# q and k in nine passes of 128 outputs, and an instruction order that counts blocks of 128 pairs

## The chip, the cores and the metric

The kernel runs on one core of a Trainium2 chip. The metric is the time of one execution on the device in microseconds; for a kernel, the median of several executions is given with the lowest and the highest. The core's engines have their own instruction streams: TensorE (PE) for matrix products, with its weight loads (PEld) beside it, VectorE (DVE), ScalarE (ACT), GpSimd (POOL) and SyncE (SP), which here issues most of the DMAs in the order in which they stand in its queue.

## The reference

Four layers on x of 2048 rows and 576 columns, each with a layer norm ahead of it and a residual sum behind it: attention A, mixer B, and both again with the same weights.

```python
def _A_ref(x, wqkv, wo):
    H = 32; Dh = D // H          # 18
    W, dil = (8, 2)
    qkv = (x @ wqkv).reshape(B, S, 3, H, Dh).transpose(2, 0, 3, 1, 4)
    q, k, v = (qkv[0], qkv[1], qkv[2])
    idx = pos[:, None] - (jnp.arange(W) * dil)[None, :]
    ...
    logits = jnp.einsum('bhsd,bhswd->bhsw', q, kg) * Dh ** (-0.5)
    attn = _softmax(jnp.where(mask, logits, -1e9))
    o = jnp.einsum('bhsw,bhswd->bhsd', attn, vg)
    return o.transpose(0, 2, 1, 3).reshape(B, S, D) @ wo
def _B_ref(x, w_in, w_sp, b_sp, w_out):
    z = _gelu(jnp.einsum('bsd,df->bsf', x, w_in))          # 4608 columns
    z1 = z[..., :Fh]
    z2 = _layernorm(z[..., Fh:], axis=-1)
    g = jnp.einsum('ts,bsf->btf', w_sp, z2) + b_sp[None, :, None]
    return jnp.einsum('bsf,fd->bsd', z1 * g, w_out)
x = x + _A_ref(_layernorm(x), A_wqkv, A_wo)
x = x + _B_ref(_layernorm(x), B_w_in, B_w_sp, B_b_sp, B_w_out)
x = x + _A_ref(_layernorm(x), A_wqkv, A_wo)
x = x + _B_ref(_layernorm(x), B_w_in, B_w_sp, B_b_sp, B_w_out)
```

A row attends to eight rows: itself and those 2, 4, ... 14 above it.

## The kernel before

There are five stages, `phase_F(0)`, `phase_S(1)`, `phase_F(2)`, `phase_S(3)` and `phase_E()`. An F stage (an attention stage, below) makes the attention layer and the half z2 of the mixer's first product, with its norm. An S stage makes z1 (`z1_ps`) and the spatial product (`g_ps`). The mixer's last product (`p_ps`, `p3_steps`) is done at the start of the following F stage, or in E for the last layer.

In an F stage the normalised input lies transposed in `xnD`: features on the partitions, in five chunks along `NM + 1`. The first four chunks are 128 features each. The last has 64 features, and they stand twice, in rows 0 to 63 and again in rows 64 to 127, so that two products of half the array's height can run side by side. That is what `mm576` does: for two outputs `s` it issues four full chunks each (8 matmuls, L246) and the half chunk of each (2 matmuls, L240), the half chunks first or last, so that two neighbours that use `mm576` can share one change between full and half height.

Attention goes over 18 tiles of 114 rows (each with a halo of 14 rows above it, 128 in all), and 9 groups of two tiles. For a group, `QK_steps` makes q and k with the outputs (32 heads of 18 = 576 each) on the partitions and the group's 242 rows as columns. It goes in five pieces `d` of 126, 126, 126, 126 and 72 outputs, seven heads or four; a piece holds q in one half of a PSUM tile `H` and k in the other. DVE or ACT copies a piece to a buffer `stg` with even and odd rows apart (`.e`), SP writes it to `qk_bounce` in DRAM (`.w`), and when all five pieces are written, four DMAs read it back as `QK` with heads side by side at partitions 0, 32, 64 and 96. Three tiles `H` in PSUM serve every matrix product of the stage in turn.

A tile then goes: `L_ps`, the logits, two steps of 32 small matmuls (18 rows, 57 columns, L516); exp on ACT (L524); the mask on DVE (L531); `O_ps`, 64 small matmuls (L539) with v (`v_ps`, 20 matmuls, L485); the division on DVE (L548); five transposes `o_tp`; `w_ps`, ten matmuls with wo (L588); the residual sum on DVE (L593); its store, its layer norm (statistics on DVE, three small operations on POOL, the scaling on ACT L277) and five transposes `ln_tp` back into `xnD`. The z2 half (`z_ps`, from L246 and L240) of 128 rows is three `mm576` steps, gelu on ACT, squares on DVE and ACT, small operations on POOL and a scaling on DVE.

Which step follows which on an engine is written out by a planner when the kernel is built. `Flow.step` records a step with its engine, an assumed cost, a due time `key`, the steps it needs (`after`) and the buffers it takes; `Flow.order` then places the steps one at a time, each time on the engine that is free first, and there the ready step with the lowest due time. Due times are tile numbers less constants in `Plan`, one set for each attention stage: `KQ` for q and k, `KV` for v, `KL` for the logits, and so on; `LX`, `LW` and `LR` are the assumed latencies of loads, of the write to `qk_bounce` and of its read. The emitted order is fixed: an engine that waits for one step holds all that stand behind it, on SP too. PE's steps in the stage are not emitted in any other order than the planner's.

Of the kernel before, what the change touches and what calls it, by code (L numbers as in the profile page):

```python
# [9 lines left out]
ACT = mybir.ActivationFunctionType  # L10
# [31 lines left out]

Plan = namedtuple("Plan", "LX LW LR KQ KX KV KL KE KM KP KF KY KZ STAY")
PLANS = (Plan(LX=6.05, LW=5.23, LR=6, KQ=5.82, KX=8.97, KV=1.81, KL=2.17, KE=1.72, KM=1.23, KP=0.96, KF=1.71, KY=1.13,
              KZ=16, STAY=0.41),
         Plan(LX=3.13, LW=3.88, LR=7.8, KQ=4.18, KX=10.88, KV=0.84, KL=1.2, KE=1.46, KM=0, KP=0.42, KF=0.82, KY=1.35,
              KZ=13.51, STAY=0.39))
# [3 lines left out]
class Flow:  # L51
# [4 lines left out]

    LAG = 0.12
    SWITCH = dict(PE=0.1, ACT=1.3)

    def __init__(self, caps, stay=0.6):  # L60
        self.caps, self.stay = caps, stay
        self.steps = []
        self.by = {}
        self.users = {}

    def step(self, name, eng, cost, key, fn, after=(), uses=(), takes=(), mode=None, lag=None):
        st = dict(name=name, eng=eng if isinstance(eng, tuple) else (eng,), cost=cost, key=key, fn=fn,
                  after=list(after), takes=takes, mode=mode, lag=self.LAG if lag is None else lag, n=len(self.steps))
# [26 lines left out]

    def order(self):
# [5 lines left out]
        while left:  # L102
            best = {}
            for st in left.values():
# [5 lines left out]
                else:  # L110
# [3 lines left out]
                    t = max(t, tk)  # L114
                    e = min(st["eng"], key=lambda e: max(free.get(e, 0.0), t))
# [21 lines left out]
            free[e] = st["end"]  # L137
            for tag, b in st["takes"]:
                taken.setdefault(tag, []).append(b)
# [14 lines left out]
class K:  # L154
# [7 lines left out]
    def __init__(self, ctx, tc, aps):  # L162
# [3 lines left out]
        self.dma_rr = 0  # L166

# [83 lines left out]
    def ln_steps(self, fl, tag, key, row0, n, x, after, uses=(), guard=()):  # L251
# [41 lines left out]
        fl.step(tag + ".t", "PE", 0.32, key, trans, [tag + ".n"], [tag + ".xn"], takes=[("PT", tag + ".tp")], mode="w")  # L293
# [9 lines left out]
    def p3_steps(self, fl, i, key, wout, x_prev, li, after=()):  # L303
# [35 lines left out]
        for hh in range(2):  # L339
            for part in range(2):  # L340
# [3 lines left out]
                        takes=[("H", tag + ".ps")] if (hh, part) == (0, 0) else [], mode="w")  # L344
# [12 lines left out]
    def phase_F(self, li):  # L357
# [11 lines left out]
        fl = Flow(dict(H=3, PT=2, QK=3, bn=2, stg=6, x=nx, xw=3, xn=3, ln_st=6, o_t=2, oT=2, xb=8), pl.STAY)  # L369
# [5 lines left out]
        wqk = pool.tile([P, NM, 2, D], bf16, name="wqk")  # L375
        wqk_r = pool.tile([P, D], bf16, name="wqk_r")
# [23 lines left out]
        def load_qk():  # L400
            self.load576(lambda s: wqk[:, :, s, :], wqk_r, self.A_wqkv[:, 0:D], self.A_wqkv[:, D:2 * D], (nc.sync,))
# [29 lines left out]
        def QK_steps(g, key):  # L431
# [5 lines left out]
            for d in range(5):  # L437
                M = 126 if d < 4 else 72

                def mm(rest_first, d=d, M=M):  # L440
                    ps = box[d] = self.Ht("qk_ps")
                    cols, at = slice(126 * d, 126 * d + M), slice(c0, c0 + gw)
                    self.mm576(lambda s: ps[:M, s, 0:gw], rest_first,
                               lambda s, c: (wqk[:, c, s, cols], self.xnD[:, c, at]),
                               lambda s, rows: (wqk_r[rows, cols], self.xnD[rows, NM, at]))

                def ev(e, d=d, M=M):
                    t = pool.tile([P, 4 * GH], bf16, name="stg", bufs=6)
                    stg = box[d, "s"] = t[:, 0:2 * gw].rearrange("p (q r j) -> p q r j", q=2, r=2)
                    self.copy(e, stg[:M], box[d][:M, :, 0:gw].rearrange("p q (j r) -> p q r j", r=2))  # L450

                def wr(_, d=d, M=M):
                    self.dma(box["bn"][126 * d:126 * d + M], box[d, "s"][:M])
                fl.step(f"{tag}.m{d}", "PE", 0.2 + 0.0039 * gw, key, mm, feeds(c0, gw) + ["wqk"],
                        takes=[("H", f"{tag}.ps{d}")], mode="wn")
                fl.step(f"{tag}.e{d}", ("DVE", "ACT"), dict(DVE=0.15 + 0.00215 * gw, ACT=0.15 + 0.0018 * gw), key, ev,
                        [f"{tag}.m{d}"], [f"{tag}.ps{d}"],
# [253 lines left out]
        with tc.manual_schedule():  # L711
            fl.issue()
# [134 lines left out]
```

## Time and profile before

| what | value |
|---|---|
| median of 3 executions | 1275.97 us (1269.72 to 1276.37) |
| the profiled execution, time | 1273.12 us |
| its span, first to last instruction | 1271.4 us |
| mean granted TensorE clock | 0.987 |
| first attention stage, to the first `z1_ps` | 0 to 245.3 us |
| first S stage | 245.3 to 565.9 us |
| second attention stage, with `p_ps` at its start | 565.9 to 874.6 us |
| second S stage and E | 874.6 to 1271.4 us |
| PE busy in the two attention stages | 230.5 of 245.3 us, 300.1 of 308.7 us |
| DVE and ACT busy in the second attention stage | 188.1 us and 159.2 us |
| share of the 16 DMA engines in the two attention stages | 0.53 and 0.49 |

A window's line has its length, the busy time of each engine with its number of instructions in brackets, the mean granted clock of PE (1.00 is full speed), the share of the DMA engines that was busy, and GB/s. In the page's groups a line of code comes with its engine, its operation, its shapes and count, the busy time with the mean duration of one, and the idle time ahead of it with what ended it. A duration of a matmul is longer than the distance to the next one, since they are pipelined; the distance is read from start to start in the timeline.

### The profile page before, as it was taken

Reading aid. Unit: us, or ns where it says so; the run is one execution under the profiler, and the core shown is the slowest. Engines: PE = TensorE matmul, PEld = TensorE weight load, DVE = VectorE, ACT = ScalarE, POOL = GpSimd, SP = SyncE. Lnnn points to the kernel's source line nnn. Section 1 sums busy time; section 2 is a strip of 40 time slices with the busy share of each in tenths; the row PEclk is TensorE's granted clock in tenths of the full one; section 3 lists DMA queues with packets and bytes.
Section 4 is the critical chain, followed back from the end, with each engine's and each line's share of the span. In section 5 each row is a group of like instructions: output and inputs, shape, how many; then the busy total and the mean of one; then the engine's idle time right before and its main releaser. Section 6 shows DMA issues by size and latency. Waiting matters only on the chain.

```text
span 1271.4 us, 27781 instructions
## 1 busy us (share of the span) xinstructions
PE 1239.1 (97%) x12182; PEld 730.5 (57%) x12244; DVE 551.9 (43%) x897; ACT 408.9 (32%) x658; POOL 201.4 (16%) x494
## 2 busy tenths in 40 slices
PE   7999999999999999999999998999999999999998
PEld 5788765444444444448788886554444444444576
DVE  5866665433222232334467675654233232322311
ACT  6566687600111111103333446875110011111011
POOL 5311157600000000002111112674000000000000
PEclk9999899999999999999999898999999999999999
DMA  7655319150000000044554455049300000000232
GB/s 192 159 149 163 95 48 199 29 129 10 10 10 10 10 10 1 1 140 147 140 141 115 113 142 161 18 105 197 83 1 10 10 10 10 10 1 2 82 101 68
DMA packets 142877, 96.31 MB, mean 76 GB/s; under 512 B 92084, under 2 KB 127604, under 8 KB 142756
## 3 DMA queue, kind: packets, MB, share of 16 engines
q1 hardware_dynamic: 142068, 92.17, 28.1%
q0 software_dynamic: 688, 2.38, 0.7%
q8 instruction: 95, 1.56, 0.5%
q14 instruction: 26, 0.21, 0.1%
HBM read 51.19 MB, written 26.55 MB: 61 GB/s over the span
## 4 chain that ended last, share of the span: by engine, by line
PE 92%; DMA 2%; ACT 2%; issue 1%; DVE 1%; POOL 0%; SPq 0%; DVEq 0%; POOLq 0%; ACTq 0%
PE g_ps L764 39%; PE z_ps L246 20%; PE p_ps L321 10%; PE qk_ps L246 6%; PE w_ps L588 4%; PE v_ps L485 3%; PE z_ps L240 3%; PE O_ps L539 3%; PE L_ps L516 1%; DMA QK<-qk_bounce 1%; PE ln_tp L283 1%; PE qk_ps L240 1%; PE o_tp L568 1%; ACT P L524 1%; DMA wqk<-in_A_wqkv_dram 1%
## 5 line engine op out<-in xcount | busy, mean ns | idle before, releaser
L764 PE MATMUL g_ps<-W,zu 128*128 128x512 bf16 x2256 | 497.7, 379 | 2.5
L764 PEld LDWEIGHTS <-zu 128*128 128x128 bf16 x2304 | 225.4, 98 | 271.9
L769 DVE TENSOR_TENSOR g_tmp<-g_ps,bsp 128x512 f32<-128x512 f32 x144 | 99.0, 687 | 437.6 <-PE g_ps L764 437.6
L759 ACT ACTIVATE zu<-z_ps 128x1024 bf16<-128x1024 f32 x72 | 73.7, 1024 | 514.4 <-PE z_ps L240 477.1
L246 PE MATMUL z_ps<-xnD,w 128*128 128x512 bf16 x562 | 132.1, 379 | 1.2 <-issue 0.6
L321 PEld LDWEIGHTS <-zu 128*128 128x128 bf16 x1152 | 111.6, 98 | 30.6 <-DVE zu L770 2.1
L246 PE MATMUL z_ps<-wA,xnD 128*128 128x384 bf16 x576 | 109.8, 327 | 0.1
L321 PE MATMUL p_ps<-wA,zu 128*128 128x288 bf16 x768 | 106.7, 286 | 0.0
L770 DVE TENSOR_TENSOR zu<-g_tmp,zu 128x512 bf16<-128x512 f32 x144 | 99.7, 692 | 9.9 <-DVE g_tmp L769 0.5
L246 PEld LDWEIGHTS <-xnD 128*128 128x128 bf16 x768 | 70.8, 98 | 56.5 <-issue 14.4
L246 PEld LDWEIGHTS <-w 128*128 128x128 bf16 x576 | 52.8, 97 | 75.2 <-issue 15.7
L246 PE MATMUL qk_ps<-xnD,wqk 128*126 128x242 bf16 (+1 forms) x720 | 90.4, 272 | 1.8 <-ACT xnD L301 0.9
L633 ACT ACTIVATE zu<-z_ps 128x768 bf16<-128x768 f32 x96 | 77.4, 806 | 35.8 <-PE z_ps L240 20.1
L643 DVE CUSTOM_DVE_ANT_1 zu<-zu 128x1536 bf16<-128x1536 bf16 x32 | 56.6, 1769 | 55.0 <-ACT zu L633 55.0
L246 PEld LDWEIGHTS <-wqk 128*126 128x126 bf16 (+1 forms) x720 | 75.1, 133 | 8.6 <-issue 6.6
L524 ACT ACTIVATE P<-L_ps 128x912 bf16<-128x912 f32 x72 | 64.8, 944 | 18.9 <-PE L_ps L516 18.8
L266 POOL TENSOR_SCALAR ln_st<-ln_st 128x1 f32<-128x1 f32 (+1 forms) x68 | 18.8, 277 | 315.6 <-DVE ln_st L262 273.4
L328 DVE TENSOR_TENSOR x<-p_ps,x 128x576 f32<-128x576 f32 x32 | 24.2, 757 | 90.6 <-PE p_ps L321 90.6
L588 PE MATMUL w_ps<-wo,oT 128*114 128x288 bf16 (+1 forms) x360 | 56.5, 309 | 0.4 <-ACT P L524 0.2
L277 ACT ACTIVATE xn<-xw,ln_st 114x512 bf16<-114x512 f32 (+1 forms) x72 | 43.0, 646 | 33.5 <-POOL ln_st L268 33.2
L300 DVE CAST stg<-qk_ps 126x484 bf16<-126x484 f32 (+1 forms) x61 | 40.3, 660 | 28.5 <-PE qk_ps L240 14.6
L588 PEld LDWEIGHTS <-oT 128*114 128x114 bf16 (+1 forms) x360 | 47.1, 142 | 4.0 <-issue 1.7
(79 smaller groups left out, 1116.1 us busy)
## 6 DMA issues: line engine op xcount, KB each, us to landing
QK<-qk_bounce SPq DMA_DIRECT2D x72, 136.1 KB
x<-xres SPq DMA_DIRECT2D x32, 288.0 KB
xres<-xw SPq DMA_DIRECT2D x34, 256.5 KB
qk_bounce<-stg SPq DMA_DIRECT2D x72, 119.1 KB
w<-in_B_w_in_dram SPq DMA_DIRECT2D x36, 128.0 KB
xres<-x SPq DMA_DIRECT2D x16, 288.0 KB
xw<-xres SPq DMA_DIRECT2D x17, 256.5 KB
wA<-in_B_w_in_dram SPq DMA_DIRECT2D x12, 288.0 KB
```

Of the source, the lines that this page charges most:

```text
L240: nc.tensor.matmul(ps(s), lhsT=lhsT, rhs=rhs, start=first, stop=not first)
L246: nc.tensor.matmul(ps(s), lhsT=lhsT, rhs=rhs, start=(c == 0 and not rest_first), stop=(c == NM - 1 and rest_first))
L277: nc.scalar.activation(out=out, in_=in_, func=ACT.Identity, scale=rstd[:n], bias=nmr[:n])
L321: nc.tensor.matmul(ps[:, hh, 0:288], lhsT=u[:, s * S + i * P:s * S + (i + 1) * P], rhs=wout(b, s)[:, hh * 288:(hh + 1) * 288], start=(b == ...
L524: nc.scalar.activation(out=Psb[:, 2 * hh:2 * hh + 2, :, 0:QH], in_=box["L", hh][:, :, 0:8 * QH].rearrange("p a (b c) -> p a b c", c=QH), f ...
L588: nc.tensor.matmul(box["ps"][:n, hh, 0:288], lhsT=box["oT"][:, c, :n], rhs=wo[:, c, hh * 288:(hh + 1) * 288], start=(c == 0), stop=(c == 4))
L633: nc.scalar.activation(out=self.zu[:, 3 * u:3 * u + 3, 256 * i:256 * (i + 1)].rearrange("p j (s r) -> p s j r", s=2), in_=box[u][:, :, 0:3 ...
L643: nc.vector.tensor_tensor_reduce(out=junk(0, 6), in0=z[:, 0:6, :], in1=z[:, 0:6, :], scale=1.0 / FH, scalar=0.0, op0=ALU.mult, op1=ALU.add ...
L759: nc.scalar.activation(out=u[:, :, 512 * q:512 * (q + 1)], in_=ps[:], func=ACT.Gelu_apprx_tanh)
L764: nc.tensor.matmul(ps[:, s, :], lhsT=z2[:, i, s, :], rhs=W[q][:, i, :], start=(i == 0), stop=(i == NS - 1))
L769: nc.vector.tensor_tensor(out=tmp[:], in0=ps[:, s, :], in1=bsp[:, 512 * q:512 * (q + 1)], op=ALU.add)
L770: nc.vector.tensor_tensor(out=uv, in0=tmp[:], in1=uv, op=ALU.mult)
```

## The change

It has two parts.

The first is in `QK_steps`. The five pieces become four passes of 128 outputs of q and the same of k, and a fifth, `qk4`, that holds the last 64 of q and the last 64 of k as one pass of 128 outputs and 242 columns. For that, the weights are laid out in another way: `wqk` has 1152 columns, q's 576, then the last 64 of k, then the first 512 of k, so that columns 512 to 639 are the last of q and the last of k. `qk4` is five matmuls of full height; its last chunk takes `wqk_r` in 128 rows, of which the lower 64 are filled with zeros by POOL (`wzero`), as the 64 features stand twice in `xnD`. The result goes to `qk_bounce` in two writes. The loads of q's and k's weights are six DMAs instead of four.

The second is in the planner. `Flow` gets a count of PE's pairs of weight load and matmul: each PE step now has `pairs`, and `Flow` holds for each block of 128 pairs when it will be there. A block is taken to be asked for at pair 80 of a stretch and needed 146 pairs later; blocks come one after the other and each takes `fetch` (4.6 and 4.5 in the two stages). A step that would reach a block before it is there is taken to start later, so another step may come first. The constants of both plans are others, and a new one, `KS`, sets the distance of the z2 tiles' due times (0.5 before).

```diff
-PLANS = (Plan(LX=6.05, LW=5.23, LR=6, KQ=5.82, KX=8.97, KV=1.81, KL=2.17, KE=1.72, KM=1.23, KP=0.96, KF=1.71, KY=1.13,
-              KZ=16, STAY=0.41),
-         Plan(LX=3.13, LW=3.88, LR=7.8, KQ=4.18, KX=10.88, KV=0.84, KL=1.2, KE=1.46, KM=0, KP=0.42, KF=0.82, KY=1.35,
-              KZ=13.51, STAY=0.39))
+PLANS = (Plan(LX=3.5, LW=5.23, LR=5.54, KQ=4.59, KX=8.53, KV=1.33, KL=2.17, KE=1.05, KM=0.91, KP=0.98, KF=1.31, KY=2.56,
+              KZ=15.38, KS=0.37, STAY=0.41, LF=4.6),
+         Plan(LX=3.13, LW=4.15, LR=7.96, KQ=4.18, KX=10.86, KV=0.84, KL=1.2, KE=0.79, KM=0.39, KP=0.42, KF=0.82, KY=2.33,
+              KZ=13.51, KS=0.47, STAY=0.49, LF=4.5))
...
+    BLOCK, PLACE, AHEAD = 128, 80, 146
...
+    def places(self, st, ahead):
+        a = self.pairs - self.PLACE - ahead
+        rate = st["cost"] / st["pairs"]
+        return [(k, (self.BLOCK * k - a) * rate) for k in range(a // self.BLOCK + 1, (a + st["pairs"]) // self.BLOCK + 1)]
...
+                    if st["pairs"]:
+                        for k, at in self.places(st, self.AHEAD):
+                            t = max(t, self.there.get(k, 0.0) - at)
...
+            if st["pairs"]:
+                for k, at in self.places(st, 0):
+                    self.there[k] = max(t0 + sw + at, self.there.get(k - 1, 0.0)) + self.fetch
+                self.pairs += st["pairs"]
...
         def load_qk():
-            self.load576(lambda s: wqk[:, :, s, :], wqk_r, self.A_wqkv[:, 0:D], self.A_wqkv[:, D:2 * D], (nc.sync,))
+            q, k0, k1 = (self.A_wqkv[:, a:b] for a, b in ((0, D), (D, D + NM * P), (D + NM * P, 2 * D)))
+            for (c0, c1), r0, r1, src in (((0, D), 0, HP, q), ((D + HP, 2 * D), HP, P, k0), ((D, D + HP), 0, HP, k1)):
+                self.dma(wqk[:, :, c0:c1], src[0:NM * P, :].rearrange("(c p) n -> p c n", p=P))
+                at = c0 if r0 == 0 else 0
+                self.dma(wqk_r[r0:r1, at:at + c1 - c0], src[NM * P:D, :])
...
-            for d in range(5):
-                M = 126 if d < 4 else 72
...
+            for d in range(NM):
+                def mm(rest_first, d=d):
+                    ps = box[d] = self.Ht("qk_ps")
+                    q, k = slice(P * d, P * d + P), slice(D + HP + P * d, D + HP + P * d + P)
+                    self.mm576(lambda s: ps[:, s, 0:gw], rest_first,
+                               lambda s, c: (wqk[:, c, (q, k)[s]], self.xnD[:, c, at]),
+                               lambda s, rows: (wqk_r[rows, q], self.xnD[rows, NM, at]))
...
+            def mm4(_):
+                ps = box[NM] = self.Ht("qk4_ps")
+                for c in range(NM + 1):
+                    lhsT = wqk[:, c, NM * P:NM * P + P] if c < NM else wqk_r[:, NM * P:NM * P + P]
+                    nc.tensor.matmul(ps[:, 0, 0:gw], lhsT=lhsT, rhs=self.xnD[:, c, at], start=(c == 0), stop=(c == NM))
...
+            def wr4(_):
+                for s in range(2):
+                    self.dma(box["bn"][NM * P:D, s], box[NM, "s"][HP * s:HP * s + HP])
...
-            Z2_steps(i, pl.KZ + 0.5 * i, [f"win2.{k}" for k in range(len(win2_parts()))] +
+            Z2_steps(i, pl.KZ + pl.KS * i, [f"win2.{k}" for k in range(len(win2_parts()))] +
```

In the order that this gives, every step of both attention stages may stand in another place; S and E are as before.

78 lines of the change are left out of this document (45 added, 33 removed).

## The prediction

> **What bounds the kernel now.** I read the page's head first, then the waits of TensorE (PE), then its timeline.
>
> ```profile
> span 1271.4 us, 27781 instructions
> PE 1239.1 (97%) x12182; PEld 730.5 (57%) x12244; DVE 551.9 (43%) x897; ACT 408.9 (32%) x658; POOL 201.4 (16%) x494
> ...
> q8 instruction: 95, 1.56, 0.5%
> ...
> PE 92%; DMA 2%; ACT 2%; issue 1%; DVE 1%; POOL 0%; SPq 0%; DVEq 0%; POOLq 0%; ACTq 0%
> ...
> L246 PE MATMUL qk_ps<-xnD,wqk 128*126 128x242 bf16 (+1 forms) x720 | 90.4, 272 | 1.8 <-ACT xnD L301 0.9
> ...
> L246 PEld LDWEIGHTS <-wqk 128*126 128x126 bf16 (+1 forms) x720 | 75.1, 133 | 8.6 <-issue 6.6
> ```
>
> PE is busy 97% of the span and is 92% of the chain that ends last, so a PE instruction less is time less, unless a wait takes its place. Queue q8 brings instructions: 95 packets, 1.56 MB, so 16.4 KB each. PE has 12,244 pairs of weight load and matmul; 12,244 / 95 is 129 pairs to a packet. That is the "block of 128 pairs" of the change. The waits of PE show what such a block can cost:
>
> ```profile
> PE L_ps L516 <- issue: 8.0, 6, 2.8
> ...
> PE L_ps L516 <- DMA QK<-qk_bounce: 2.6, 3, 1.2
> ```
>
> "issue" is idle time with no semaphore behind it. One of the six, in the timeline of PE (start, time, work):
>
> ```profile
> 84.51 0.47 PE L516 MATMUL L_ps<-QK 18*64 18x57 bf16 x36
> 86.40 0.41 PE L516 MATMUL L_ps<-QK 18*64 18x57 bf16 x28 [1.42 <-issue]
> ...
> 88.50 2.65 PE L588 MATMUL w_ps<-wo,oT 128*114 128x288 bf16 x10
> 90.94 0.74 PE L568 MATMUL o_tp<-ident,o_t 128*128 128x128 bf16 x5
> ```
>
> PE stops in the middle of a step that waits for nothing. I numbered PE's pairs in the built program's order: the gaps end at pairs 735, 1503, 2782, 7773, 8157, 8669 (O_ps) and 9181, all 93 to 95 past a multiple of 128. They are late instruction blocks: 0.40 + 1.42 + 1.61 + 0.72 + 1.05 + 0.21 + 2.81 = 8.2 us. After five of them the clock falls (windows; PEclk is after POOL's count):
>
> ```profile
> 88.00:92.00 4.00, 4.00 (x55) 3.72 (x50) 2.96 (x5) 1.26 (x3) 0.00 (x0) 0.57 0.40 91
> 140.00:147.00 7.00, 7.00 (x99) 5.42 (x98) 3.83 (x7) 2.73 (x5) 1.86 (x3) 0.54 0.23 59
> 713.00:720.00 7.00, 7.00 (x104) 5.58 (x104) 4.38 (x8) 2.15 (x4) 1.86 (x3) 0.51 0.48 104
> 734.00:738.00 4.00, 4.00 (x73) 3.06 (x72) 2.55 (x3) 0.51 (x1) 0.00 (x0) 0.63 0.36 80
> 777.00:782.00 5.00, 5.00 (x36) 3.82 (x35) 2.45 (x5) 2.14 (x3) 0.50 (x1) 0.56 0.58 157
> ```
>
> Length x (1 - clock) is what each loses: 1.7 + 3.2 + 3.4 + 1.5 + 2.2 = 12.0 us; PE looks fully busy there, but the w_ps step above takes 2.44 us (88.50 to 90.94). So the gaps cost some 20 us, 8.2 as idle and 12 as slow clock.
>
> **The change, part by part.** First q and k. A piece now, from the timeline:
>
> ```profile
> 121.93 1.43 PE L588 MATMUL w_ps<-wo,oT 128*114 128x288 bf16 x10
> 123.20 0.44 PE L568 MATMUL o_tp<-ident,o_t 128*128 128x128 bf16 x5
> 123.48 0.99 PE L246 MATMUL qk_ps<-xnD,wqk 128*126 128x242 bf16 x8
> 124.41 0.42 PE L240 MATMUL qk_ps<-xnD,wqk_r 64*126 64x242 bf16 x4
> 124.76 1.04 PE L246 MATMUL qk_ps<-xnD,wqk 128*126 128x242 bf16 x8
> 125.64 1.39 PE L588 MATMUL w_ps<-wo,oT 128*114 128x288 bf16 x10
> ```
>
> Two pieces run from 123.48 to 125.64, so 1.08 us each; the fifth, of 72 outputs, has the same ten matmuls and columns and costs the same. The change keeps four and replaces the fifth by qk4: five matmuls of full height, with no change to half height. A w_ps step of ten matmuls of 288 columns takes 1.27 us (121.93 to 123.20), 127 ns each; 242 columns by proportion 107 ns, five 0.53 us. Bounds: 0.50 (nothing under the columns' share) to 0.67 (five weight loads of 133 ns, not overlapped). A group saves 1.08 - 0.53 = 0.55 us (0.41 to 0.58); 9 groups in each of two attention stages: **9.9 us** (7.4 to 10.4), all of it PE time on the chain.
>
> Weight loads get shorter too: 133 ns at 126 columns, 98 at 128 (the row of `<-xnD` loads). I count nothing for it: a wide matmul follows the one before in about 107 ns although its load takes 133, so the loads overlap. [...]
>
> The fifth eviction shrinks from 484 columns (660 ns on DVE) to 242, between 330 and 660 ns: nothing on the path, since DVE is busy 188.1 of the 308.7 us of the second attention stage. Without that cover it would be a gain of at most 18 x 0.33 = 6 us. The bounce to DRAM has six writes for five, 18 issues more at 0.3 us on SP, and 640 packets for 576 in a group; the reads stay. That lies under the distance from a group's last q/k pass to its first L_ps (second rival). The weights come in six DMAs instead of four: two issues of 0.55 us stand ahead of the x_in loads on SP, in the first stage where PE waits 6.9 us for the first normalised rows: **+1.1 us** (0 to 2.5, if the 64-column piece lands late too). In the second stage they lie under the 320 us before it. POOL's fill of wqk_r's lower half falls into its 2.8 us of idle before 4.16 us: nothing.
>
> Then the order, which moves every step of both attention stages, with their loads and stores on SP. I counted in both built orders how much PE work stands between the place where a block is asked for and the pair that needs it. The diff puts these 146 pairs apart, from pair 80 on; the gaps, 93 to 95 past the multiple, put the first at 77 to 80. Steps are costed by the timeline: L_ps 0.33, O_ps 1.0, v_ps 1.36, w_ps 1.25, qk_ps 1.08, z_ps 1.57, p_ps 0.1225 a pair, transposes 0.28. With 3.9 us for a block (my fit) the shortfalls of the order before are 0.5, 0.9, 0.9, 1.7, 0.5, 1.2 in the first stage and 0.7, 1.7, 0.3, 0.3 in the second: 8.6 us, against the measured 8.2. The order after has four stretches under 3.9 us: 3.34 in the first stage, 2.98, 3.29 and 3.11 in the second, shortfall 0.6 + 0.9 + 0.6 + 0.8 = 2.9 us. Six stretches were under 3.3 us, three are now. So idle falls by 8.2 - 2.9 = 5.3 us. Lost clock I scale with it, 12.0 x 2.9 / 8.6 = 4.0, a gain of 8.0. Together **13.3 us**. Bounds: 0 (blocks arrive as late wherever they fall; the one behind the gap that ends at 776.13 came 6.8 us after its place) to 20.
>
> [...]
>
> New waits: the last group of the first stage has 11.5 us of PE work between its last pass and its first L_ps (18.0 before). In the quiet part of that stage the way took about 12: write issued at 129.87, reads issued from 134.80 to 136.66, landed some 4 us later by the packets of the trace. **+1.0 us** (0 to 4). The activation table is loaded twice more (1.28 us each) on ACT, which is 32% busy: nothing; if not hidden, 2.6.
>
> Sum: -9.9 + 1.1 - 13.3 + 1.0 = -21.1. Span 1271.4 - 21.1 = 1250.3; the profiled execution's time, 1273.12, lies 1.7 above its span: 1252. It is 2.9 below the median of 1275.97 (1269.72 to 1276.37), so I add 1: **1253 us**.
>
> **The rivals.** (1) The blocks come as late as before, because other DMA traffic and not PE's pace decides. For: the block at 773 took 6.8 us with the 16 DMA engines 0.79 busy. Against: most gaps stand where the stretch is short. Then 1271.4 - 9.9 + 2.1 + 1.7 + 1 = 1266, less what short stretches still bring: 1263.
>
> (2) Slower: q and k reach L_ps too late. In the first stage the distances fall from 18 to 30 us (groups 2 to 8) to 11.5 to 18.4. The last group of the second stage needed about 21 us before (eviction at 764.0, L_ps released at 784.97, because its write stood on SP behind an xw load until 769.80). If the way takes 19 us everywhere, groups of the first stage wait 5.3 + 2.9 + 0.6 + 2.3 + 2.2 + 1.6 + 4.0 + 4.2 + 7.5 = 31 us, of the second 9: 1253 + 40 = 1293. It outweighs the gain from a way of about 17.5 us on. Against: in all of before PE waited 2.6 us for these reads, with group 0 on its way for about 15 us at its busiest.
>
> (3) Weight loads set the pitch: 35 ns on 810 loads, 28 us more: 1225. Against: the 107 ns above.
>
> (4) All gaps go: 1253 - 6.9 = 1246.
>
> (5) The passes save nothing, since half-height switches or qk4's wait for its eviction eat the 0.55 us a group: 1263. Against: pieces of 128 outputs stream the same columns.
>
> **How the numbers follow.** Forecast (1246 to 1260) 0.55; (1) 0.16; (2) in part or whole 0.10, of which 0.06 end above +0.5%; (3) 0.03; (4) 0.10; (5) 0.06. The range 1242 to 1268 holds 8 in 10: it takes in (1), (4), (5) and a small (2). Faster by over 0.5% (under 1269.6; half a per cent is about what a measurement of this kernel tells from no change) 0.87, within 0.07, slower 0.06.
>
> **What would show it.** Right: PE has 90 pairs less; qk4 takes about 0.53 us; "issue" on PE in the attention stages falls to about 3 us, in the second stage mostly; fewer windows with a clock near 0.5; p_ps, g_ps and the tail unchanged. Wrong: PE waits on `QK<-qk_bounce` above 5 us, gaps of "issue" that stay at 8 us, or qk4 near 1 us.

## The result and the profile after

The changed kernel takes 1265.26 us (median of 7 runs, 1260.96 to 1267.65) against 1275.97 us (7 runs, 1269.72 to 1281.72): a ratio of 0.9914, 95% interval 0.9889 to 0.994. It is faster, by 10.7 us; the forecast said 23. The profiled execution took 1265.77 us, with a span of 1264.0. First the page's head, the instruction queue, the chain and the two groups of q and k:

```profile
span 1264.0 us, 27640 instructions
PE 1228.7 (97%) x12092; PEld 712.2 (56%) x12154; DVE 541.5 (43%) x886; ACT 414.9 (33%) x671; POOL 201.2 (16%) x496
...
q8 instruction: 95, 1.56, 0.5%
...
PE 91%; DMA 3%; DVE 1%; ACT 1%; issue 1%; SPq 1%; POOL 0%; DVEq 0%; ACTq 0%; POOLq 0%
...
L269 PE MATMUL qk_ps<-xnD,wqk 128*128 128x242 bf16 x576 | 72.0, 272 | 3.1 <-ACT xnD L324 0.8
...
L269 PEld LDWEIGHTS <-wqk 128*128 128x128 bf16 x576 | 54.3, 99 | 13.6 <-issue 8.0
```

PE has 90 weight loads fewer (12,154 for 12,244) and 10.4 us less busy time, and it is still the chain. A load of q's and k's weights takes 99 ns for 133, while a matmul keeps its 272 ns. The span fell by 7.4 us, so some of what PE no longer does came back as idle time. The waits of PE (total, times, longest) show where:

```profile
PE ln_tp L306 <- ACT xn L300: 7.1, 3, 6.3
PE L_ps L566 <- DMA QK<-qk_bounce: 6.3, 7, 1.6
PE L_ps L566 <- DVE stg L323: 3.7, 1, 3.7
PE p_ps L344 <- DVE zu L822: 1.5, 2, 0.8
PE L_ps L566 <- issue: 1.4, 1, 1.4
PE L_ps L566 <- ACT P L574: 1.1, 1, 1.1
...
PE v_ps L535 <- issue: 0.7, 1, 0.7
...
PE O_ps L589 <- issue: 0.4, 1, 0.4
```

"issue" in the attention stages is down to 1.4 + 0.7 + 0.4 = 2.5 us, from 8.2. In its place stand 6.3 us on the reads of q and k (2.6 before) and 3.7 us on one eviction. Then the clock. These windows hold every stretch at half clock but one in the program's last 2 us; a line has length, busy times, granted clock, DMA share, GB/s:

```profile
33.70:40.50 6.80, 5.10 (x127) 3.73 (x127) 4.88 (x11) 2.27 (x3) 3.45 (x8) 0.50 0.87 197
47.40:54.20 6.80, 6.79 (x95) 5.33 (x94) 3.00 (x4) 2.15 (x3) 0.00 (x0) 0.50 0.24 57
153.20:156.60 3.40, 3.40 (x31) 2.88 (x27) 2.64 (x4) 1.63 (x3) 0.00 (x0) 0.50 0.38 137
753.90:760.70 6.80, 5.37 (x61) 3.97 (x62) 1.79 (x2) 0.97 (x2) 0.00 (x0) 0.50 0.60 191
774.40:781.20 6.80, 6.43 (x113) 4.03 (x114) 2.15 (x3) 4.29 (x6) 0.52 (x2) 0.50 0.42 146
```

They last about 31 us together. Before there were six such stretches (from 33.8, 88.5, 139.7, 713.1, 733.6 and 774.5 us), also about 31 us. So there are five for six, at other steps of the program, and the time at half clock is the same.

For every run I made the same account over the two attention stages: their lengths; PE's idle time (gaps over 0.06 us) and what of it is "issue"; the time at half clock (granted clock 0.50), which costs half its length; and what is left, PE's work at full clock. A stage ends here where the first `z_ps` matmul of the next stage starts (243.4 us in before, 1.9 us ahead of the 245.3 in the table of the section on the time before). Where a kernel has extra matmuls, they are taken off (2.25 us for ten). The ratio is of several executions, the rest of a row of one.

| kernel | ratio to before (95%) | stages | idle | issue | half clock | work |
|---|---|---|---|---|---|---|
| before, five pieces | 1 | 243.4 + 306.8 | 23.2 | 8.4 | 30.8 | 511.6 |
| after | 0.9914 (0.9889 to 0.994) | 241.6 + 301.1 | 25.9 | 2.4 | 30.8 | 501.4 |
| after, once more | 0.9914 (0.9886 to 0.9942) | 242.0 + 301.1 | 27.9 | 1.9 | 27.3 | 501.6 |
| e1: nine passes, constants of before | 0.9971 (0.9946 to 0.9997) | 245.9 + 306.2 | 34.4 | 5.8 | 37.6 | 498.9 |
| e2: five pieces, planner of after | 1.0083 (1.006 to 1.0105) | 245.7 + 319.6 | 32.5 | 14.9 | 40.9 | 512.4 |
| e3: after, reads assumed longer | 0.9939 (0.9917 to 0.9961) | 235.3 + 306.0 | 27.1 | 5.7 | 23.9 | 502.3 |
| e3b: the same, by less | 0.9909 (0.9885 to 0.9932) | 237.5 + 305.0 | 25.2 | 2.5 | 30.8 | 501.9 |
| e5: nine passes, order of before | 0.9955 (0.9929 to 0.9981) | 240.8 + 306.0 | 28.0 | 4.9 | 37.6 | 500.0 |
| e6: five pieces, order of after | 0.9937 (0.9916 to 0.9957) | 239.2 + 305.0 | 22.4 | 2.2 | 13.6 | 515.0 |
| e7: reads longer in the first stage | 0.9894 (0.9865 to 0.9923) | 240.8 + 302.1 | 27.3 | 4.6 | 23.9 | 503.7 |
| e8: win2 loads earlier | 0.9891 (0.9865 to 0.9917) | 239.7 + 300.6 | 25.5 | 1.4 | 23.9 | 502.9 |
| e9: e8, and reads longer in both | 0.9921 (0.9895 to 0.9947) | 239.4 + 301.9 | 26.2 | 4.0 | 27.3 | 501.5 |
| e10: five pieces, order of e9 | 1.001 (0.9988 to 1.0031) | 241.1 + 308.3 | 23.4 | 2.1 | 20.5 | 515.8 |
| e11: e7 and e8 together | 0.9912 (0.9882 to 0.9941) | 241.0 + 300.0 | 28.8 | 6.1 | 17.0 | 503.7 |
| e12: after, waits filled | 0.9881 (0.9852 to 0.991) | 233.5 + 305.6 | 19.0 | 4.0 | 17.1 | 502.5 |
| e13: e8, waits filled | 0.9872 (0.9838 to 0.9905) | 235.1 + 299.6 | 18.8 | 3.0 | 10.2 | 504.0 |
| e14: five pieces, order of e13 | 0.9953 (0.9938 to 0.9969) | 241.3 + 305.0 | 18.8 | 3.1 | 6.8 | 517.4 |
| e15: e13 once more | 0.9889 (0.9871 to 0.9907) | 233.2 + 303.1 | 21.4 | 7.7 | 6.8 | 504.7 |
| e16: two DVE steps exchanged | 0.9896 (0.9864 to 0.9928) | 237.4 + 301.8 | 23.3 | 1.3 | 27.4 | 502.2 |
| e17: e13 with that exchange | 0.9866 (0.9811 to 0.9921) | 238.1 + 299.0 | 21.4 | 3.6 | 13.6 | 504.4 |

From before to after: work -10.2, issue -6.0, other idle +8.7, lost clock 0.0; together -7.5, which is what the two stages lost (1.8 + 5.7). The other stages (322.5, 322.5 and 76.4 us) didn't change. A gap inside a slow stretch counts twice in this account, as idle and as lost clock (1.6 us of such gaps in before, 3.5 in after); counted once, the work fell by 9.3 us and the lost clock by 1.0.

How far one execution's row can be trusted is seen where the same program, or the same stage, ran twice. The changed kernel's two rows differ by 2.0 us of idle and 3.5 of half clock, e13's and e15's by 4.7 us of issue. The first stage has one plan in after, after once more and e8 (241.6, 242.0 and 239.7 us) and one in e3 and e7 (235.3 and 240.8 us): up to 5.5 us of difference in one stage is chance.

### The profile page after: what moved, and what is told of

It reads as the page before. It is cut to its first block, busy times and chain, and to the rows that moved or that the text cites. A ratio compares the mean times of both kernels' runs of the same rounds, so it can differ in the third digit from the quotient of the medians.

```text
span 1264.0 us, 27640 instructions
## 1 busy us (share of the span) xinstructions
PE 1228.7 (97%) x12092; PEld 712.2 (56%) x12154; DVE 541.5 (43%) x886; ACT 414.9 (33%) x671; POOL 201.2 (16%) x496
## 4 chain that ended last, share of the span: by engine, by line
PE 91%; DMA 3%; DVE 1%; ACT 1%; issue 1%; SPq 1%; POOL 0%; DVEq 0%; ACTq 0%; POOLq 0%
PE g_ps L816 39%; PE z_ps L269 20%; PE p_ps L344 10%; PE qk_ps L269 4%; PE w_ps L638 4%; PE z_ps L263 3%; PE v_ps L535 3%; PE O_ps L589 3%; PE L_ps L566 2%; DMA QK<-qk_bounce 2%; PE ln_tp L306 1%; DMA qk_bounce<-stg 1%; DMA x_in<-in_A_x_dram 1%; PE o_tp L618 1%; SPq L192 1%
## 5 line engine op out<-in xcount | busy, mean ns | idle before, releaser
L269 PE MATMUL qk_ps<-xnD,wqk 128*128 128x242 bf16 x576 | 72.0, 272 | 3.1 <-ACT xnD L324 0.8
L289 POOL TENSOR_SCALAR ln_st<-ln_st 128x1 f32<-128x1 f32 (+1 forms) x68 | 18.9, 277 | 290.0 <-DVE ln_st L285 237.5
L269 PEld LDWEIGHTS <-wqk 128*128 128x128 bf16 x576 | 54.3, 99 | 13.6 <-issue 8.0
L269 PE MATMUL z_ps<-wB,xnD 128*128 128x384 bf16 x192 | 47.3, 328 | 0.0
```

The lines of the kernel that those rows point to most:

```text
L269: nc.tensor.matmul(ps(s), lhsT=lhsT, rhs=rhs, start=(c == 0 and not rest_first), stop=(c == NM - 1 and rest_first))
```

## The experiments

**The two parts alone, replanned.** e1 has the passes with the constants and the planner of before, e2 the five pieces with the planner and constants of after:

```diff
 # e1, against after: constants of before in both plans, KS=0.5, LF=0.0 (no block is ever late)
-PLANS = (Plan(LX=3.5, LW=5.23, LR=5.54, ..., KS=0.37, STAY=0.41, LF=4.6), ...
+PLANS = (Plan(LX=6.05, LW=5.23, LR=6, ..., KS=0.5, STAY=0.41, LF=0.0), ...
 # e2, against after: QK_steps, load_qk and the layout of before
-            for d in range(NM):
+            for d in range(5):
+                M = 126 if d < 4 else 72
```

> The nine passes of the change with the constants of before and no block count (the planner still makes its own order from them). My theory: the passes give their 9.9 us whatever the order, and the order of the change gave back to q/k waits and slow clock what it won from late blocks. Its order is short of blocks by 2.2 + 1.8 us at 3.9 us a block (before 5.6 + 3.0, after 0.6 + 2.3), and the last five groups of the second stage have 14.5 to 22.7 us from their last pass to their first L_ps. Expected: 1262 to 1268. Rival: the passes give 3 us or less and the order the rest: 1272 or more. Other rival: the order costs, and the passes give more than the whole: under 1261.

> The five pieces of before in the planner of the change, with its constants and its block count. My theory: idle on issue falls (its order is short by 4.7 + 2.2 us, before 5.6 + 3.0), waits for q and k rise (11.8 to 18.2 us in the first stage), so 1270 to 1278, ratio 0.995 to 1.003. Rival (the order gives the gain and the passes little): 1264 to 1268. Other rival (the order costs): 1280 or more.

1271.17 and 1286.79 us, both slower than I expected. Neither is the change's half: with other costs the planner makes another order. e2's idle on issue is 14.9 us, the most of all, one gap alone 5.4 us, although its planner counts blocks as after's does. Constants found for nine passes don't carry to five pieces; the parts had to be told apart with the order held.

**The two parts alone, each in a held order.** In e5 the nine passes stand where the pieces stood in before's PE order (`qk4` is planned with the fifth piece's cost); in e6 the five pieces stand where the passes stand in after's:

```diff
 # e5, against after, beside before's constants
-            fl.step(f"{tag}.m{NM}", "PE", 0.05 + 0.0021 * gw, key, mm4, feeds(c0, gw) + ["wqk", "wzero"],
-                    takes=[("H", f"{tag}.ps{NM}")], mode="w", pairs=5)
+            fl.step(f"{tag}.m{NM}", "PE", 0.2 + 0.0039 * gw, key, mm4, feeds(c0, gw) + ["wqk"],
+                    takes=[("H", f"{tag}.ps{NM}")], mode="wn")
 # e6, against after, beside before's pieces
+                fl.step(f"{tag}.m{d}", "PE", 0.2 + 0.0039 * gw if d < 4 else 0.05 + 0.0021 * gw, key, mm, ...
+                        takes=[("H", f"{tag}.ps{d}")], mode="wn" if d < 4 else "w", pairs=10 if d < 4 else 5)
```

> The nine passes alone, each step of PE in the same place as in the kernel before (the planner is told the costs of before): qk4 stands where the fifth piece stood. My theory: the passes are worth their 9.9 us in PE time, less some 1 us for the two more loads at the start; late blocks stay (short by 4.6 + 2.6 us at 3.9 us a block, before 5.6 + 3.0, since 45 pairs less a stage move the places): 1263 to 1269, ratio 0.990 to 0.995. Rival: PE time saved in a pass comes back as waits close behind it, as in e1_passes (ratio 0.997): 1270 to 1274. In the profile: qk4 near 0.53 us, waits for q and k as in before (2 to 4 us).

> The five pieces of before, each step of PE in the same place as in the changed kernel. Against the changed kernel (1265) it takes the passes away and nothing else of the order. My theory: 9.9 us more PE time, and distances to L_ps 0.5 us longer: 1272 to 1278, ratio to before 0.997 to 1.003. Rival (the order alone brings most of the gain): 1265 to 1269.

1270.5 and 1266.32 us: both times fall to the rival, not to my theory. The passes alone are worth 0.45%, the order alone 0.63%, both 0.86%. The account shows that the passes took 11.6 us of PE work out of before's order and 13.6 out of after's; in both they also brought idle (+4.8 and +3.5 us) and half clock (+6.8 and +17.2 us).

**Longer assumed reads.** The latency that the planner assumes for reading q and k back (`LR`) is raised, from 5.54 and 7.96:

```diff
-PLANS = (Plan(LX=3.5, LW=5.23, LR=5.54, ...), Plan(LX=3.13, LW=4.15, LR=7.96, ...))
+PLANS = (Plan(LX=3.5, LW=5.23, LR=9.0, ...), Plan(LX=3.13, LW=4.15, LR=11.5, ...))   # e3
+PLANS = (Plan(LX=3.5, LW=5.23, LR=8.0, ...), Plan(LX=3.13, LW=4.15, LR=10.0, ...))   # e3b
+PLANS = (Plan(LX=3.5, LW=5.23, LR=9.0, ...), Plan(LX=3.13, LW=4.15, LR=7.96, ...))   # e7
```

> The change with another assumed latency of the read of q and k (LR 9.0 and 11.5 instead of 5.54 and 7.96): L_ps comes later behind its group's passes, at least 15.7 us in the first stage (11.5 before the edit) and 17.2 in the second (15.2). My theory: waits of PE on QK<-qk_bounce, some 10 us with the wait at 35.4, fall under 3 us, and slow clock behind them with them: 1252 to 1260. Rival: the waits move to another place (exp, eviction, the z2 tiles at the end), since the work that can stand in between runs out: 1263 to 1268. Its order is short of blocks by 2.1 + 2.8 us, so idle on issue may be 2 us more than in the change.

> As e3_lr with LR 8.0 and 10.0: distances at least 14.1 us in the first stage and 16.1 in the second, blocks short by 0.6 + 1.5 us. My theory: between the change and e3_lr in q/k waits (3 to 6 us), least idle on issue of the four: 1254 to 1262. Rival: 1263 to 1268.

> The change with the longer assumed latency of the read in the first attention stage alone (LR 9.0 instead of 5.54); the second stage's plan is the change's. In e3_lr the first stage took 235.3 us (241.6 in the change) and the second 306.0 (301.1), with waits of z_ps for wA. My theory: the first stage keeps its gain and the second stays: 1256 to 1262. Rival (what the first stage wins is chance of one execution, its order being short of blocks by 2.1 us): 1263 to 1268.

1268.15, 1264.29 and 1261.37 us; the first two miss my theory. e3's first stage is 6.3 us shorter than after's, with 3.4 us at half clock for 17.1, but in its second stage PE waits 4.4 us for `wA` and the stage is 4.9 us longer. Raised in the first stage alone (e7) it gains a little, an interval that overlaps after's. Its time is in the range of my theory, but its reason is not borne out: the first stage, planned as in e3, took 240.8 us in e7's profile, so most of e3's 6.3 us was chance. The waits for q and k can be planned away (neither first stage has one), but then others come: 4.4 us for `wA` in e3, and in both first stages 2.1 us on an eviction and 1.3 to 1.4 us for `wo`.

**The loads beside the reads.** In the second stage the reads of group 7 are issued from 745.25 to 747.14 us on SP and the loads of `win2` (`wA`, `wB`) right behind them; PE stands in the middle of the logits meanwhile (timelines of SP and PE in the changed kernel):

```profile
745.25 1.89 SPq L192 DMA_DIRECT2D QK<-qk_bounce  x4
747.18 0.38 SPq L192 DMA_DIRECT2D wA<-in_B_w_in_dram  x1
747.61 1.07 SPq L192 DMA_DIRECT2D wB<-in_B_w_in_dram  x2
```

```profile
752.41 0.44 PE L566 MATMUL L_ps<-QK 18*64 18x57 bf16 x31 [0.53 <-DMA QK<-qk_bounce]
754.50 0.25 PE L566 MATMUL L_ps<-QK 18*64 18x57 bf16 x1 [1.65 <-DMA QK<-qk_bounce]
755.58 0.64 PE L566 MATMUL L_ps<-QK 18*64 18x57 bf16 x31 [0.82 <-DMA QK<-qk_bounce]
...
758.60 2.47 PE L638 MATMUL w_ps<-wo,oT 128*114 128x288 bf16 x10
```

The last read lands at 755.58, 8.4 us after its issue. Half clock begins at 753.9, inside the second of the waits of 0.53, 1.65 and 0.82 us (the fourth window above), and the w_ps step behind them takes 2.39 us, from 758.60 to 760.99. e8 issues the `win2` loads two tiles earlier, after which the planner also exchanges some of PE's steps near the end of the second stage; e9 adds longer reads in both stages; e10 is e9's order with five pieces; e11 joins e7 and e8:

```diff
-            fl.step(f"win2.{k}", "SP", 0.45, 0, f, [f"a{3 + k if first else min(11 + k // 2, NT - 1)}.L"] +
+            fl.step(f"win2.{k}", "SP", 0.45, 0, f, [f"a{3 + k if first else min(9 + k // 2, NT - 1)}.L"] +
```

> The change with the loads of win2 in the second attention stage (and there alone) set free two tiles earlier (after tile 9 + k//2 instead of 11 + k//2); the first stage is the change's. The reads of q and k of the last two groups landed 8.4 us after their last issue in the change, with up to four such loads of 288 KB right behind them. Theory A (the loads are what makes these reads late): waits on QK in the second stage fall from 5.6 us to under 2, and with their slow clock the time by 4 to 8 us: 1257 to 1261. Theory B (SP's order does it: the writes stand behind loads of xw that wait for a buffer): waits stay at 4 to 6 us and the time at 1263 to 1267.

> The change with both findings together: the longer assumed latency of the read (LR 8.0 and 11.5) and win2's loads in the second stage two tiles earlier. Distances at least 14.1 us in the first stage and 17.2 in the second (the last two groups 21.3 and 35.3), blocks short by 0.6 + 1.5 us at 3.9 us a block. My theory (waits for q and k and the slow clock behind them ate half of the gain): the fastest so far, 1254 to 1260. Rival (e7 and e8 gained by one and the same few us at the end of the second stage, and other waits take over): 1260 to 1264.

> The five pieces of before in exactly the order of e9_longer. It tells what the passes are worth where hardly anything waits for q and k. Theory A (PE is the bound, the passes save 9.9 us of it, and waits for q and k took it back in the order of before and of the change): 8 to 11 us above e9_longer. Theory B (in these stages a quarter to a half of PE's saved time is always lost, since other chains set the pace of the first 35 us and of the stretches with late blocks): 2 to 6 us above. Its order is short of blocks by 4.1 + 2.9 us, so 3 to 4 us of a difference can be late blocks rather than passes; the profile tells them apart.

> e7_lr_first and e8_win2 in one: LR 9.0 in the first stage, win2's loads two tiles earlier in the second. Each alone was 2 to 5 us faster than the change (1261.4 and 1260.2). If their gains are of different stages they add: 1255 to 1259. If they are the spread of one and the same kernel's executions: 1260 to 1264.

1260.2, 1264.68, 1275.58 and 1263.44 us. In e8 the waits for q and k in the second stage fall from 5.6 to 3.2 us, between Theory A's 2 and Theory B's 4. The time is in Theory A's range, but the second stage is only 0.5 us shorter, and the first, which the edit doesn't touch, 1.9 us. So that the loads make these reads late is not shown. In e9 no wait for q and k is left, but 2.4 us for `wA`, 2.7 on an eviction and 4.0 of issue came in, and a stretch of 17.1 us at half clock begins at 37.1, behind that eviction (35.17, in the first stage); its time is above both ranges. Between e9 and e10 the passes are worth 0.9%, 10.9 us: all that the forecast gave them. e11's gains don't add: group 7 waits 4.9 us again and one issue gap is 2.3 us.

The changed kernel ran once more beside these:

> The changed kernel itself on the same chip as the two above: 1262 to 1267.

1264.49 us, with the same ratio, the same waits (6.3 us for q and k, 4.2 on the eviction) and 27.3 us of half clock for 30.8.

**Filling a wait.** e12 puts ten matmuls of 512 columns ahead of the first logits step of groups 0 and 8 in the first stage and 7 and 8 in the second. Their result is overwritten by the logits; nothing else differs.

```diff
+FILL = ((0, 8), (7, 8))
+                    if a == 0 and t == t0s[group[t]] and group[t] in FILL[0 if first else 1]:
+                        for _ in range(10):
+                            nc.tensor.matmul(ps[:, 0, :], lhsT=self.ident[:], rhs=wqk[:, 0, 0:512], start=True, stop=True)
```

> The changed kernel, with ten extra matmuls of 512 columns (about 2.2 us) on PE ahead of the first L_ps of four groups whose wait for q and k it showed (groups 0 and 8 of the first stage, 7 and 8 of the second); their result is overwritten. The steps stand in the same places. Theory A (the clock falls because PE idles, and three of the five slow stretches of the change begin at these waits): the slow stretches at 34, 754 and 774 us go or shrink, each worth up to 3.4 us of PE time, so 1255 to 1261. Theory B (the clock falls for another reason, or the waits only move): as the change, 1263 to 1268. If the extra work is not covered by the wait it costs up to 8.8 us: 1268 to 1274.

1260.65 us. The place of after's longest wait, first in after and then in e12 (PE's timeline), and below them e12's window of it:

```profile
31.28 0.45 PE L566 MATMUL L_ps<-QK 18*64 18x57 bf16 x32 [0.28 <-ACT stg L324]
35.40 0.92 PE L566 MATMUL L_ps<-QK 18*64 18x57 bf16 x64 [3.68 <-DVE stg L323]
36.26 1.25 PE L306 MATMUL ln_tp<-ident,xn 128*128 128x128 bf16 x10
37.43 2.13 PE L535 MATMUL v_ps<-wv,xnD 128*64 128x288 bf16 x16
```

```profile
30.53 2.32 PE L565 MATMUL L_ps<-wqk,ident 128*128 128x512 bf16 x10 [0.23 <-ACT stg L325]
32.78 0.45 PE L570 MATMUL L_ps<-QK 18*64 18x57 bf16 x32
34.04 0.70 PE L570 MATMUL L_ps<-QK 18*64 18x57 bf16 x64 [0.81 <-DVE stg L324]
34.67 0.73 PE L307 MATMUL ln_tp<-ident,xn 128*128 128x128 bf16 x10
35.33 1.17 PE L536 MATMUL v_ps<-wv,xnD 128*64 128x288 bf16 x16
```

```profile
33.70:40.50 6.80, 6.46 (x220) 5.17 (x219) 4.84 (x12) 5.96 (x9) 4.63 (x10) 1.00 0.87 185
```

With the wait filled, the same v_ps takes 1.17 us for 2.13, and PE is at it 2.1 us earlier although it did 2.25 us more. The whole first stage has no half clock left (17.1 us in after) and is 8.1 us shorter: its idle fell by 4.9 us, the fill took 4.5, and half of the 17.1 us, 8.6, came back as clock; 0.9 us went elsewhere. It isn't chance: the first stage with this fill took 233.5, 235.1 and 233.2 us (e12, e13, e15), without it 241.6, 242.0 and 239.7 (after, after once more, e8). So the clock fell behind PE's waits on q and k and on an eviction as it had behind late blocks, and in the first stage wide matmuls in their place kept it; the last section counts the work around such places. The second stage is 4.5 us longer: its two fills took 4.5 us and saved only 2.0 us of idle, and it has 17.1 us at half clock for 13.7, 10.2 of them behind a late block of 2.25 us that ends at 719.05.

**Filled and earlier, and the passes once more.** e13 is e8 with the fill at groups 0 and 8 of the first and 7 of the second stage; e14 is the same order with five pieces; e15 is e13 again.

> e8_win2 with the same ten matmuls ahead of groups 0 and 8 of the first stage and group 7 of the second. Theory A: 1251 to 1257, the fastest; theory B: 1260 to 1264.

> The kernel of e13 (win2 loads two tiles earlier, ten matmuls of 512 columns whose result is overwritten ahead of three first logits steps) with the five pieces of before in place of the nine passes; every PE step stands where it stands there. Theory A (the passes save 0.55 us of PE time a group, 18 x 0.55 = 9.9 us, and it shows in full wherever PE doesn't wait and the clock isn't cut; in the order of the changed kernel itself it was eaten by waits for q and k and slow clock): 9 to 11 us slower than e13, so 1266 to 1269 at a ratio to before near 0.995, with qk4 back at ten matmuls. Theory B (the passes are worth only the 1 to 2 us that the same-order comparison in the order of the changed kernel gave): 1258 to 1260.

> e13 once more, in more rounds: Theory A (PE's waits filled and the clock kept): a ratio to before of 0.985 to 0.990, below the 0.9914 of the changed kernel. Rival (e13 was only a good draw): 0.990 to 0.994, the same as the changed kernel.

1257.47, 1267.9 and 1259.41 us; e13 lies just above its Theory A, far from Theory B. e14 against e15, on the same chip: the passes are worth 8.5 us, a little under Theory A's 9 to 11 and far from Theory B's 1 to 2. So in these two orders the passes' time comes out almost in full; in the other two pairs idle and clock took half of it or more back. e15's interval (0.9871 to 0.9907) lies on Theory A's side, but still overlaps after's own.

**What the longest wait waited for.** I had called the 3.68 us above a wait for q and k. DVE's timeline in the changed kernel says otherwise, and SP's says why:

```profile
28.11 0.66 DVE L323 CAST stg<-qk_ps 128x484 bf16<-128x484 f32 x1 [0.19 <-PE qk_ps L269]
33.66 0.92 DVE L284 BATCH_NORM_STATS2 ln_st<-x_in 128x6 f32<-128x288 bf16 x2 [4.89 <-DMA x_in<-in_A_x_dram]
34.61 0.21 DVE L285 BATCH_NORM_AGGREGATE ln_st<-ln_st 128x2 f32<-128x12 f32 x1
34.74 0.61 DVE L323 CAST stg<-qk_ps 128x484 bf16<-128x484 f32 x1
```

```profile
25.21 1.67 SPq L192 DMA_DIRECT2D QK<-qk_bounce  x4
26.98 0.95 SPq L192 DMA_DIRECT2D x_in<-in_A_x_dram  x2
28.02 0.50 SPq L192 DMA_DIRECT2D qk_bounce<-stg  x1
28.57 4.00 SPq L192 DMA_DIRECT2D QK<-qk_bounce  x4
```

A load of x_in is issued behind group 0's reads and lands at 33.66, some 6 us after its issue. DVE stands 4.89 us in front of it, and behind it in DVE's queue stands the eviction of a q/k piece that PE had long finished (in e16 it starts at 29.18). That eviction frees the PSUM tile which the logits step needs. The chain is load, DVE, PSUM tile, PE. In the first 60 us DVE waited 3.4 us for x_in before and 11.6 now; `LX`, the latency assumed for these loads, went from 6.05 to 3.5. That `LX` is what makes the load late is argued: no run sets it back alone. e16 exchanges the two neighbours on DVE and nothing else; e17 is e13 with this exchange in place of the fill at group 0.

```diff
-        for st in self.order():
+        out = self.order()
+        n = [st["name"] for st in out]
+        if "qk2.e2" in n and "lnx12.s" in n:
+            a, b = n.index("lnx12.s"), n.index("qk2.e2")
+            out.insert(a, out.pop(b))
+        for st in out:
```

> The changed kernel with two neighbours on DVE exchanged in the first attention stage: group 2's third q/k eviction, ready at 30.4 us, now stands ahead of a layer norm's statistics, whose input load landed only at 33.7 us; every other engine's order is untouched. PE's 3.7 us wait at 35.4 us is put down to this eviction, since the logits step needs the PSUM tile that it frees. I called this wait one for q and k in the expectation of e12. Theory A (the load of x_in, issued later since LX went from 6.05 to 3.5, holds DVE, DVE holds the PSUM tile, and that holds PE): the wait falls below 1 us, the 6.8 us of half clock behind it mostly go, and the first stage gets 3 to 7 us shorter than the 241.6 of the changed kernel; ratio to before 0.985 to 0.989. Theory B (group 0's or 1's q and k land late and the name of the eviction is only the last semaphore): PE stands until 35 us as before, then put down to QK<-qk_bounce, and the ratio stays at 0.991. Theory C (the same late x_in catches PE a step later, at the transposes of the layer norm): the idle moves and the gain is under 2 us.

> e13 with the exchange of e16 in place of the ten extra matmuls at group 0 of the first stage (win2 loads two tiles earlier; extra matmuls, overwritten, at group 8 of the first and group 7 of the second stage stay). Theory A: as fast as e13 and e15 or up to 3 us faster, 1255 to 1259 at a ratio of 0.985 to 0.988, since a wait that is taken away needs no filling. Rival (it was the extra PE work that kept the clock in the first stage, and the exchange doesn't): the half clock near 34 us is back and it is 3 us or more slower than e13 and e15, 1262 or above.

1261.51 and 1257.76 us. e16's PE at the place:

```profile
30.85 0.45 PE L571 MATMUL L_ps<-QK 18*64 18x57 bf16 x32
31.55 0.21 PE L571 MATMUL L_ps<-QK 18*64 18x57 bf16 x1 [0.26 <-DMA QK<-qk_bounce]
32.55 0.70 PE L571 MATMUL L_ps<-QK 18*64 18x57 bf16 x63 [0.79 <-DMA QK<-qk_bounce]
```

The wait of 3.68 us is gone and the logits are done 3 us earlier; the reads of q and k, which had lain behind it, now hold PE for 1.05 us. The stage is 4.2 us shorter, which is within chance. Theory A's chain from load to PE is shown by the wait; its hope that the half clock would mostly go is not: 3.4 us still begin at 34.0, behind that remaining wait, and 6.8 at 44.3, behind a wait of 1.44 us for the division on DVE. The ratio, 0.9896, is just above A's range. e17 takes the time that its Theory A gave (1257.76), though 3.4 us of half clock near 34 are back, as its rival said.

## Why the prediction was right and wrong

The sign was right, the time lies in the wide range, and the passes and the rarer late blocks brought what was forecast for them; but the gain was less than half of the forecast, since the clock gave nothing and new waits took most of the rest. By its steps:

- **Passes, -9.9:** right. The timeline of the changed kernel, with the next pass behind `qk4`:

```profile
16.31 0.28 PE L263 MATMUL qk_ps<-xnD,wqk_r 64*128 64x242 bf16 x2
16.52 0.59 PE L496 MATMUL qk_ps<-xnD,wqk 128*128 128x242 bf16 x4
16.95 0.27 PE L496 MATMUL qk_ps<-xnD,wqk_r 128*128 128x242 bf16 x1
17.05 0.99 PE L269 MATMUL qk_ps<-xnD,wqk 128*128 128x242 bf16 x8
```

 `qk4` takes 16.52 to 17.05, the 0.53 us of the forecast. PE's work fell by 10.2 us (9.3 with gaps counted once). With the order held it is 11.6 to 14.3 in the four pairs (before and e5, e6 and after, e10 and e9, e14 and e13), or 11.0 to 13.3; what lies above 9.9 may be changes between half and full height, which the fifth piece needs and `qk4` doesn't. That is argued, not shown.
- **Start, +1.1:** nothing. Up to its first passes PE idled 7.9 us before and 7.7 now; the longer issue on SP was hidden by the wait for the first normalised rows.
- **Idle on late blocks, -5.3:** right, -6.0. But I predicted it from single blocks (four short stretches), and single blocks don't repeat, as the last section shows. The sum came out, not the places.
- **Lost clock, -8.0:** the step that failed: "Lost clock I scale with it". It was tied to the block gaps alone. In e12 it followed other waits too: with the wait filled, the first stage's 17.1 us at half clock went. The late blocks' slow stretches did go (none of the five now stands behind one), and the new waits began as much of their own. Half clock is 30.8 us in both profiles. The term was also read short: the windows in the prediction end inside the five stretches, which lose 13.7 us and not 12.0, and a sixth, from 33.8 us behind a wait for q and k, loses 1.7 more. That one already spoke against tying the clock to the blocks alone.
- **New waits, +1.0:** measured +8.7, the second step that failed; waits for q and k are at 6.3 us, past the prediction's own sign of being wrong. I looked at one place, the last group of the first stage, with q and k's way as the only cause. The waits came at the start of the first stage, through DVE (3.7 us, e16), and at groups 7 and 8 of the second (5.6 us for q and k). The smaller `LX` stood in the diff, and I gave it no price.

Miss: 8.0 of clock + 7.7 of waits - 0.7 - 0.3 - 1.1 = 13.6, against 21.1 - 7.4 = 13.7 on the span.

Of the rivals, (1) named 1263, next to the measured 1265, by the wrong way: blocks came less late, not as late. (2) was right that q and k are late, at 6.3 us and not 40. (4) fell with the waits. (5) would look right from after and e6 (0.23% apart), but e9 and e10, e14 and e15 refute it: the passes' time is real, and waits and clock ate part of it. (3) is refuted by the work: about 10 us less, not 10 + 28.

Without the 8.0 us of clock my sum would have given 1261, nearer the time, but by luck: the clock gained nothing because new slow stretches took the place of the old ones, not because short gaps were harmless here. Of the five slow stretches in the trace of the changed kernel one began in a gap of 3.68 us, the other four in or behind waits of 0.5 to 1.7 us.

The versions furthest ahead of the changed kernel's 0.9914 by their ratios are e17 (0.9866), e13 and its repeat e15 (0.9872, 0.9889) and e12 (0.9881). All beat the kernel before; no single interval is clear of after's, so how much they beat the changed kernel stays open.

## What to carry to other kernels

Where PE is the bound, price a wait at its idle time plus half of the slow stretch behind it, and give the clock back only when all idling near it goes, or wide matmuls stand in its place (in e12 none of the first stage's 17.1 us at half clock was left); taking away one cause of it wasn't enough (e16: the wait of 3.68 us gone, 1.05 us of waits left, and 3.4 us of half clock behind them). PE time saved ahead of a wait on another engine turned into a longer wait (e5: 11.6 us less work, 4.8 us more idle); so look at what every queue holds back before counting the saving (SP's loads, and DVE, which stood 4.89 us in front of one of them with a finished piece behind it). To tell a shape from an order apart, hold the order: replanned halves of a change (e1, e2) say little about it. And compare one stage between two runs only when you know how far the same stage differs from run to run.

## What the runs showed of the hardware

**Half clock came in units of 3.41 us.** The stretches in the attention stages are 3.41, 6.83 or 10.24 us long, in three runs 13.65 or 17.07 (e3, e3b, e9). In each of the twenty profiles all of them start on one grid with this step; in before, those from 33.84, 88.45, 139.65, 713.09, 733.57 and 774.53 us lie 16, 15, 168, 6 and 12 steps apart.

**The clock followed the work ahead of such a step, not idling alone.** For each step of the grid around the attention stages (24 to 250 and 565 to 880 us) I counted the multiply-adds (rows x outputs x columns) of the matmuls that PE began in the 3.41 us ahead of it (the count ends 0.1 us before its start). 3.41 us full of the S stages' `g_ps` matmuls (49 in 10.74 us) hold 131 million; the line turned out near a third of that. 3029 steps follow one at full clock. 83 of them are at half clock, and 76 of these had less than 44 million ahead of them; of the 2946 others 2938 had that or more. A slow stretch ended at the same line: 46 of the 54 steps that stayed slow had less ahead of them, 81 of the 83 that came back to full clock had more. So in these traces a gap went with slow clock where narrow matmuls stood around it: the late block of 1.37 us at 141.78 in the changed kernel cost none (62 million), while 1.05 us of waits in e16 did (40 million). Ten matmuls of the fill are 84 million by themselves. And a slow stretch could go on without idling: the last two steps of e9's had no idle ahead of them, but only 42 and 40 million. This is a count over these traces, with a line fitted to them (all 25 exceptions lie between 37 and 51 million); no kernel was built to test it.

**Late blocks had fixed places and a changing choice.** That PE's issue gaps are late instruction blocks is a reading of the trace's packets: in the first S stage of before PE began 122 to 128 recorded matmuls from the start of one 16,384-byte packet of q8 to the next, and its seven issue gaps in the attention stages end 1.3 to 1.6 us behind the end of such a packet, the three in the changed kernel 1.4 to 1.6 us. I numbered PE's pairs in all twenty profiles: every issue gap over 0.15 us in the attention stages ends 90 to 95 past a multiple of 128, whatever step stands there. Which blocks are late changes between two executions of one program: in the changed kernel pairs 2910, 3038 and 9052 (1.4, 0.4, 0.7 us), and in its repeat 2014, 8156 and 8284 (0.6, 0.4, 0.8). e13 lost 3.0 us at three blocks, the same program in e15 7.5 us at six. What sets a block's way is open; the planner's fixed time for it can only lower the odds.
